# Turning q in 64x64 transposes for two more groups, and two stores sent out as one transfer each

## The chip, the cores and the metric

The kernel runs on one core of a Trainium2 chip. A core has five engines, each with its own queue of instructions: TensorE (PE in the profile, with its weight loads as PEld), VectorE (DVE), ScalarE (ACT), GpSimd (POOL) and SyncE (SP). SP only issues transfers; 16 DMA engines carry these out. The engines wait for each other and for transfers by semaphores. The metric is the device time of one execution in microseconds (us); less is better. The numbers of a profile come from one profiled execution, the times from runs of their own.

## The reference: linear attention, then a gated channel mix

The inputs q, k and v have 8 batches, 8 heads, 576 positions and 64 columns in float32. The two stages, cut to their core:

```python
# attention
q_s = softmax(q, over the 64 columns)
k_s = softmax(k, over the 576 positions)
kv  = einsum('bhsd,bhse->bhde', k_s, v)
x   = einsum('bhsd,bhde->bhse', q_s, kv)      # then heads side by side: [8, 576, 512]
# channel mix
xk = mu_k * x + (1 - mu_k) * x_prev           # x_prev: x one position earlier, zero at first
xr = mu_r * x + (1 - mu_r) * x_prev
k  = relu(xk @ w_k)                           # 512 -> 1024
v  = (k * k) @ w_v                            # 1024 -> 512
out = sigmoid(xr @ w_r) * v
```

## The kernel before

**Attention by groups.** Four heads of one batch make a group, so there are 16 groups, written (b, g) with batch b from 0 to 7 and g 0 or 1. A tile of a group holds two heads side by side in its 128 partitions (64 each) and nine blocks of 64 columns for each of two head pairs; position 9p + j stands in partition p, block j. For each group ACT takes the exponentials of q and k, DVE sums and scales q to `qs`, and ACT casts v. TensorE then needs q turned, with the 64 columns of a head along the partitions, because the product with kv contracts over them.

**Three ways of turning q.** Groups of batches 5 to 7 (`CROSSBAR`) turn it with a transposing transfer that SP issues (L516). All others use TensorE: `transpose_q` (L362 to L369) multiplies by an identity. Its loop runs over the nine blocks j, over column parts `u` and over the two partition halves `r`. For groups named in `WHOLE` (L36) there is one part of 128 columns, so 18 transposes that use 64 rows and all 128 columns of the array. For the others there are two parts of 64 columns, so 36 transposes, each in a quarter of the array. The result is the same. The halves r go to two banks of PSUM, from where ACT copies the turned q to `qt` (`copy_qt`).

**Blocks on TensorE.** From batch 1 on, the transposes and the 36 products of `kv` (L396) for one group form one block of TensorE's queue. Where the group before has its x still to compute, those products (L536, tile `w` and `qt`) are put ahead into the same block, named B; a block without them is named TKV. The first groups of batches 2 and 3 have TKV blocks (TKV20 and TKV30), the second ones B blocks (B21 and B31). The x of the last group stands alone as X71; it reads `qt_c`, which the crossbar transfer qt71 writes.

**Channel mix by units.** The 4608 rows of x are worked in ten units of 512 or 256 positions. A unit has eight products with w_k (k.., L620), ReLU on ACT (L607), a square on DVE (L611), and then for each tile m of 128 rows: the gate's product (r.., L652), tanh on ACT into a buffer `th` (L657), the product with w_v (v.., L672), and on DVE the gating into the same buffer (o.., L678). The stores (st.., L688) follow.

**A tile's stores.** The first 64 partitions of a tile hold one column block j of a batch and the last 64 the next one. In the output their rows lie nine rows apart, so the function `store` sends each half on its own: 64 rows of 2 KB, 128 KB. A tile of unit 6 has the stores st60 and st60.2, st61 and st61.2, and so on. All go through SP's queue, but for some of the last unit, which ACT issues.

**What sets the order.** Nothing is scheduled automatically. `graph` makes the operations with their dependencies; the text `ORDER` lists every operation's name, with the number of the buffer that it takes after a colon, and each engine runs its operations in that order. There are seven `th` buffers (a to g). In unit 6 the tile st60 is in th_b, st61 in th_f, st62 in th_e and st63 in th_g. SP's order there is: st60, st61, st62, st63 (two transfers each), the crossbar transfer qt71, and then unit 7's stores. th_f and th_e are taken again by unit 8's tanh.

The lines that the change meets:

```python
WHOLE = ((0, 0), (0, 1), (1, 0), (1, 1), (2, 0), (3, 0))
...
for u in ((slice(0, 128),) if (b, g) in WHOLE else two):
...
jb = (RING * half + c) // 64 + i
bb, j = jb // J, jb % J
dst = bass.AP(tensor=kn.out.tensor, offset=kn.out.offset + (bb * S + j) * C + part.start,
              ap=[[J * C, 64], [1, width]])
```

Of the kernel before, what the change touches and what calls it, by code (L numbers as in the profile page):

```python
# [16 lines left out]
B, H, S, D = 8, 8, 576, 64  # L17
C = H * D
F = 1024
J = S // 64  # L20
CT = C // 128
FT = F // 128
RING = 4 * S
# [9 lines left out]
XO = 368  # L33

FILLS = 22
WHOLE = ((0, 0), (0, 1), (1, 0), (1, 1), (2, 0), (3, 0))  # L36
FUSED = (0, 1)
EARLY_UNITS = 2
ALONE = ((2, 1), (B - 1, 1))
CROSSBAR = tuple((b, g) for b in range(5, B) for g in range(2))  # L40
FIRST = ((0, 0), (0, 1), (1, 0), (1, 1))

ORDER = """
# [57 lines left out]
sc6010:1 relu64:1 mix600 k66:0 sq62 edge61 relu65:2 sq63 k67:2 diff61:0 relu66:0 r60:1 sq64  # L101
sc6100:2 relu67:1 sc6101 r61:3 sq65 th60:1 mix610 v600:0 sq66 th61:5 sc6011 sq67 v610:2 sc6110:0
sc6111 mix601 v601 mix611 v611 rz70:2 w70:1 r62:1 o60 o61 st60 r63:3 th62:4 st60.2 v620:0 st61
th63:6 st61.2 v630:2 v621 v631 o62 k70:1 st62 o63 st62.2 k71:3 relu70:2 st63 st63.2 k72:0 sq70:1
relu71:0 qt71:2 k73:2 sq71 relu72:1 k74:1 sq72 relu73:2 k75:3 sq73 relu74:0 k76:0 sq74 relu75:1
k77:2 sq75 relu76:2 r70:1 sq76 relu77:0 B71:0.1 sq77 th70:0 v700:3 xb70:0 rz71:0 w71:2 r71:0 v701
th71:3 xs70 v710:2 o70 edge70 X71:1.0 st70 diff70:1 v711 xb71:1 st70.2 sc7000:2 r72:1 sc7001 xs71
o71 r73:0 edge71 st71 th72:2 mix700 st71.2 v720:3 diff71:0 th73:1 sc7010:1 v730:2 sc7100:0 sc7101
sc7110:2 v721 mix710 sc7111 v731 sc7011 o72 k80:1 mix711 st72 k81:0 st72.2 o73 relu80:1 mix701
st73 k82:3 relu81:2 st73.2 sq80:0 k83:2 sq81 relu82:0 k84:1 sq82 relu83:1 k85:0 sq83 relu84:2  # L110
k86:3 sq84 relu85:0 k87:2 sq85 relu86:1 r80:1 sq86 relu87:2 r81:0 sq87 th80:5 v800:3 th81:4 v810:2
v801 v811 o80 r82:1 st80 o81 st80.2 r83:0 th82:6 st81 st81.2 v820:3 th83:0 v830:2 v821 v831 o82
k90:1 st82 o83 k91:0 st82.2 relu90:0 k92:3 st83 relu91:1 sq90:1 k93:2 relu92:2 sq91 st83.2 k94:1
relu93:0 sq92 k95:0 relu94:1 sq93 k96:3 relu95:2 sq94 k97:2 relu96:0 sq95 r90:1 relu97:1 sq96 sq97
r91:0 th90:3 v900:3 th91:2 v901 v910:2 o90 v911 st90.2 st90 v910.2:1 o91 v911.2 st91.2 st91 o91.2
st91.4 st91.3
"""


# [16 lines left out]
class Plan:  # L136
# [6 lines left out]
    def add(self, engine, emit, deps=(), takes=(), gives=(), name=""):  # L143
        self.names[name] = self.names.get(name, 0) + 1
        if self.names[name] > 1:
            name = f"{name}.{self.names[name]}"
        op = Op(engine, emit, deps, takes, gives, name)
        self.ops.append(op)
        return op
# [29 lines left out]
def graph(kn):  # L179

    plan = Plan()
    add = plan.add
# [93 lines left out]
    def emit_rest():  # L276
# [10 lines left out]
        out=kn.mu[:], in_=kn.bank(mu_slot)[:, 0:8]), [mu_mm], [], [mu_slot], name="mucopy")  # L287
# [10 lines left out]
    def weight(dst, src, n, ct, step, count, col):  # L298
# [5 lines left out]
                    name=f"wk{h}{g}") for g in range(2)] for h in range(2)]  # L304
    wr_done = add("POOL", lambda: weight(kn.wr, kn.w_r, C, 0, 1, CT, 0), name="wr")
    wv_done = [add("POOL", lambda i=i, a=a, e=e: weight(kn.wv[i], kn.w_v, C, a, 1, e - a, 0),
                   name=f"wv{i}") for i, (a, e) in enumerate(zip(WV, WV[1:]))]
# [7 lines left out]
    def attention(b, g):  # L315
# [46 lines left out]
        def transpose_q(slot):  # L362
            for j in range(J):
                for u in ((slice(0, 128),) if (b, g) in WHOLE else two):
                    for r in range(2):
# [58 lines left out]
        for n, u in enumerate(us):  # L424
# [7 lines left out]
            elif n == 0:  # L432
                castv.append(vdone[g])
        crossed = (b, g) in CROSSBAR
        before_t, before_kv = scaled + [identity], expk + castv + [consts]
# [155 lines left out]
    def wv_of(ft):  # L591
        i = max(i for i in range(3) if WV[i] <= ft)
        return kn.wv[i][:, ft - WV[i]]

    def unit(half, c0, n, index):
# [30 lines left out]
        for f0 in range(0, FT, 4 if early else 1):  # L626
            step = 4 if early and f0 == 0 else 1
            for f1 in range(f0, f0 + (4 if early else 1), step):
                kfs = [Slot("mm") for _ in range(step)]
                mms = [None] * step  # L630
                for cts in ((0, 2), (1, 3)) if step == 4 else ((0, 2, 1, 3),):
                    gs = sorted({ct % 2 for ct in cts})
                    for i in range(step):
# [5 lines left out]
                                     name=f"k{index}{fc}")  # L639
# [5 lines left out]
        for m in range(tiles):  # L645
            c = c0 + 128 * m
            rps, th = Slot("mm"), Slot("th")
            parts = [slice(0, 256), slice(256, 512)] if last and m == tiles - 1 else [slice(0, C)]

            def r_part(rps=rps, c=c):  # L650
                for ct in range(CT):
                    kn.nc.tensor.matmul(kn.bank(rps), lhsT=kn.xs[1][:, ct, c:c + 128],  # L652
                                        rhs=kn.wr[:, ct, :], start=(ct == 0),
                                        stop=(ct == CT - 1))

            def tanh(rps=rps, th=th):
                kn.nc.scalar.activation(out=kn.ths[th.index][:], in_=kn.bank(rps),  # L657
                                        func=ACT.Tanh, scale=0.5)

            own = sorted({4 * half + c // S, 4 * half + (c + 127) // S})  # L660
            r = add("PE", r_part,
                     [o for b in own for g in range(2) for o in mixed[b, g, 1]] + [wr_done],
                     [rps], [], name=f"r{index}{m}")
            rdone.append(r)
            t = add("ACT", tanh, [r], [th], [rps], name=f"th{index}{m}")
            for part in parts:
                vps = Slot("mm")
                width = part.stop - part.start

                def v_part(fts, vps=vps, m=m, part=part, width=width):  # L670
                    for ft in fts:
                        kn.nc.tensor.matmul(kn.bank(vps)[:, 0:width],  # L672
                                            lhsT=kn.k2s[k2.index][:, ft, 128 * m:128 * m + 128],
                                            rhs=wv_of(ft)[:, part], start=(ft == 0),
                                            stop=(ft == FT - 1))

                def gated(vps=vps, th=th, part=part, width=width):
                    kn.nc.vector.scalar_tensor_tensor(  # L678
                        out=kn.ths[th.index][:, part], in0=kn.ths[th.index][:, part],
                        scalar=1.0, in1=kn.bank(vps)[:, 0:width], op0=ALU.add, op1=ALU.mult)  # L680

                def store(i, queue, th=th, c=c, part=part, width=width):
                    jb = (RING * half + c) // 64 + i
                    bb, j = jb // J, jb % J
                    dst = bass.AP(tensor=kn.out.tensor,
                                  offset=kn.out.offset + (bb * S + j) * C + part.start,
                                  ap=[[J * C, 64], [1, width]])
                    kn.queues[queue].dma_start(  # L688
                        out=dst, in_=kn.ths[th.index][64 * i:64 * (i + 1), part])

                o = None
                cuts = WV if index == 0 else (0, 4, 8)
                for h, (a, e) in enumerate(zip(cuts, cuts[1:])):
                    o = add("PE", lambda v=v_part, a=a, e=e: v(range(a, e)),
                             squares[a:e] + [o or r] + [wv_done[i] for i in range(3)
                                                        if WV[i] < e and WV[i + 1] > a],
                             [] if a else [vps], [k2] if e == FT else [], name=f"v{index}{m}{h}")
                o = add("DVE", gated, [o, t], [], [vps], name=f"o{index}{m}")
                for i in range(2):
                    queue = "ACT" if last and m >= tiles - 2 and i else "SP"  # L700
                    add(queue, lambda i=i, q=queue, f=store: f(i, q), [o], [], [th],
                        name=f"st{index}{m}")
        units_of[half, c0] = (bs, kdone, rdone)

    index = 0
    for half in range(B // 4):
        for c0, n in UNITS:
            unit(half, c0, n, index)
            index += 1
# [128 lines left out]
```

## Time and profile before

| what | number |
|---|---|
| median of 3 runs | 196.36 us (195.99 to 196.37) |
| the profiled execution's own time | 195.85 us |
| its span, first to last instruction | 194.1 us |
| TensorE busy | 185.5 us (96%), 1849 products |
| VectorE, ScalarE, GpSimd busy | 150.0, 140.5, 43.6 us |
| DMA | 41.86 MB, mean 216 GB/s |
| chain that ended last | PE 77%, DMA 15%, POOL 2%, ACT 2%, issue 1% |

A busy share is over the whole span. A row of a timeline gives start, duration, engine, line, operation, tiles (out<-in), the part of the array used (rows*columns), the shape and how many. TensorE's products are pipelined, so a group's row reaches into the next one's; how long a group holds the queue is read from one start to the next. On SP a row is the issue of a transfer, not the transfer itself. The share of DMA in a stretch is the mean over 16 engines of the time that their packets took.

### The profile page before, as it was taken

The page shows a single profiled execution, that of the slowest core. Times are in us where ns is not written, and L with a number is a line of the kernel's source. Part 1 is how long each engine was busy: PE and PEld are TensorE (multiplying, and loading weights), DVE is VectorE, ACT ScalarE, POOL GpSimd, SP SyncE. Part 2 cuts the span into 40 slices and gives each one's busy share as a digit, 9 for nine tenths or more (in the row PEclk, how much of TensorE's full clock was granted, in tenths as well). Part 3 has the DMA queues.
Part 4 walks back from the last instruction along what each step waited for, and adds up shares of the span by engine and source line. Part 5 has one row for each costly group of instructions (what it writes and reads, how often), then busy time and mean ns, then how long its engine had stood idle before and what let it go on. Part 6 is the DMA issues. An engine that isn't in the chain of part 4 may idle for free.

```text
span 194.1 us, 4743 instructions
## 1 busy us (share of the span) xinstructions
PE 185.5 (96%) x1849; PEld 90.6 (47%) x1873; DVE 150.0 (77%) x347; ACT 140.5 (72%) x218; POOL 43.6 (22%) x70
## 2 busy tenths in 40 slices
PE   7989999999999999999999999999999999999991
PEld 2264445435544554554554444444444444444751
DVE  1897668799999999999989998999924469622531
ACT  3687889899999999989996798767225641752440
POOL 8444357794414212241110000000000000000000
PEclk9999999999999999999999999999999999999999
DMA  6999999999999998899699504786049122404413
GB/s 205 312 265 289 269 349 303 400 394 393 411 391 394 392 414 339 290 351 326 145 229 120 205 0 107 163 200 147 0 110 138 34 54 54 111 0 98 93 27 108
DMA packets 23646, 41.86 MB, mean 216 GB/s; under 512 B 9404, under 2 KB 12744, under 8 KB 23624
## 3 DMA queue, kind: packets, MB, share of 16 engines
q0 software_dynamic: 9440, 27.99, 45.3%
q1 hardware_dynamic: 13368, 12.13, 25.8%
q10 hardware_dynamic: 816, 1.44, 2.0%
q8 instruction: 14, 0.23, 0.5%
q14 instruction: 8, 0.07, 0.1%
HBM read 33.56 MB, written 9.44 MB: 222 GB/s over the span
## 4 chain that ended last, share of the span: by engine, by line
PE 77%; DMA 15%; POOL 2%; ACT 2%; issue 1%; DVE 0%; POOLq 0%
PE mm_c L672 10%; PE mm_d L672 9%; PE mm_c L620 8%; PE mm_b L620 7%; PE mm_a L620 7%; PE mm_b L652 7%; PE mm_d L620 6%; DMA wk_ab<-in_moe_w_k_dram 6%; PE mm_a L672 5%; DMA wv_a<-in_moe_w_v_dram 5%; PE mm_b L672 4%; DMA raw_k<-in_v_dram 4%; PE mm_a L652 4%; PE mm_d L652 3%; PE mm_c L652 1%
## 5 line engine op out<-in xcount | busy, mean ns | idle before, releaser
L672 PEld LDWEIGHTS <-k_a 128*128 128x128 bf16 x144 | 13.7, 98 | 16.7 <-issue 0.5
L652 PEld LDWEIGHTS <-xr 128*128 128x128 bf16 x144 | 13.9, 98 | 16.2 <-issue 0.2
L672 PEld LDWEIGHTS <-k_b 128*128 128x128 bf16 x152 | 14.4, 98 | 15.0 <-issue 0.2
L652 PE MATMUL mm_b<-wr,xr 128*128 128x512 bf16 x62 | 16.3, 379 | 0.1
L620 PEld LDWEIGHTS <-wk_ab 128*128 128x128 bf16 x80 | 7.6, 97 | 8.3 <-issue 0.8
L620 PEld LDWEIGHTS <-wk_bb 128*128 128x128 bf16 x80 | 7.8, 98 | 7.7
L620 PEld LDWEIGHTS <-wk_aa 128*128 128x128 bf16 x80 | 7.4, 98 | 8.2 <-issue 0.9
L620 PEld LDWEIGHTS <-wk_ba 128*128 128x128 bf16 x80 | 7.5, 98 | 7.9 <-DMA wk_ba<-in_moe_w_k_dram 0.2
L652 PE MATMUL mm_a<-wr,xr 128*128 128x512 bf16 x35 | 9.2, 380 | 0.1
L672 PE MATMUL mm_c<-wv_a,k_a 128*128 128x512 bf16 x32 | 8.2, 379 | 0.0
L607 ACT ACTIVATE rel_b<-mm_b 128x512 bf16<-128x512 f32 (+1 forms) x7 | 4.0, 572 | 4.9 <-PE mm_b L620 4.8
L607 ACT ACTIVATE rel_a<-mm_b 128x512 bf16<-128x512 f32 (+1 forms) x8 | 4.6, 570 | 3.9 <-PE mm_b L620 3.6
L620 PE MATMUL mm_c<-xk,wk_aa 128*128 128x512 bf16 (+1 forms) x26 | 7.3, 363 | 0.0
L611 DVE TENSOR_TENSOR k_a<-rel_b 128x512 bf16<-128x512 bf16 (+1 forms) x14 | 5.3, 380 | 2.5 <-ACT rel_b L607 2.5
L672 PE MATMUL mm_d<-wv_a,k_b 128*128 128x512 bf16 x26 | 7.1, 379 | 0.1
L652 PE MATMUL mm_d<-wr,xr 128*128 128x512 bf16 x28 | 7.2, 379 | 0.0
L620 PE MATMUL mm_c<-xk,wk_ab 128*128 128x512 bf16 (+1 forms) x24 | 6.9, 362 | 0.0
L611 DVE TENSOR_TENSOR k_b<-rel_a 128x512 bf16<-128x512 bf16 (+1 forms) x14 | 5.5, 391 | 1.8 <-ACT rel_a L607 1.3
L607 ACT ACTIVATE rel_c<-mm_a 128x512 bf16<-128x512 f32 (+1 forms) x11 | 6.0, 550 | 0.7 <-PE mm_a L620 0.7
L611 DVE TENSOR_TENSOR k_b<-rel_b 128x512 bf16<-128x512 bf16 (+1 forms) x14 | 5.5, 391 | 1.3 <-ACT rel_b L607 0.9
L611 DVE TENSOR_TENSOR k_b<-rel_c 128x512 bf16<-128x512 bf16 (+1 forms) x12 | 4.7, 391 | 1.9 <-ACT rel_c L607 1.6
L620 PE MATMUL mm_d<-xk,wk_bb 128*128 128x512 bf16 (+1 forms) x22 | 6.1, 360 | 0.1
(352 smaller groups left out, 532.5 us busy)
## 6 DMA issues: line engine op xcount, KB each, us to landing
out_dram<-th_b SPq DMA_DIRECT2D x12, 128.0 KB, 3.8
out_dram<-th_g SPq DMA_DIRECT2D x12, 128.0 KB, 2.4
out_dram<-th_d SPq DMA_DIRECT2D x11, 128.0 KB, 8.7
out_dram<-th_a SPq DMA_DIRECT2D x10, 128.0 KB, 2.8
out_dram<-th_f SPq DMA_DIRECT2D x10, 128.0 KB, 2.4
raw_k<-in_v_dram POOLq DMA_DIRECT2D x2, 576.0 KB, 9.0
raw_c<-in_q_dram POOLq DMA_DIRECT2D x2, 576.0 KB, 7.0
raw_b<-in_q_dram POOLq DMA_DIRECT2D x2, 576.0 KB, 10.3
```

Of the source, the lines that this page charges most:

```text
L607: kn.nc.scalar.activation(out=kn.rels[rel.index][:, 0:n], in_=kn.bank(kf)[:, 0:n], func=ACT.Relu, scale=HALF_ROOT)
L611: kn.nc.vector.tensor_tensor(out=kn.k2s[k2.index][:, fc, 0:n], in0=kn.rels[rel.index][:, 0:n], in1=kn.rels[rel.index][:, 0:n], op=ALU.mult)
L620: kn.nc.tensor.matmul(kn.bank(kf)[:, 0:n], lhsT=kn.wk[fc // 4][ct % 2][:, ct // 2, (fc % 4) * 128: (fc % 4) * 128 + 128], rhs=kn.xs[0][:, ...
L652: kn.nc.tensor.matmul(kn.bank(rps), lhsT=kn.xs[1][:, ct, c:c + 128], rhs=kn.wr[:, ct, :], start=(ct == 0), stop=(ct == CT - 1))
L672: kn.nc.tensor.matmul(kn.bank(vps)[:, 0:width], lhsT=kn.k2s[k2.index][:, ft, 128 * m:128 * m + 128], rhs=wv_of(ft)[:, part], start=(ft == ...
```

## The change

Two edits. First, (2, 0) and (3, 0) leave `WHOLE`, so the blocks TKV20 and TKV30 turn q in 36 transposes of 64x64 instead of 18 of 64x128. Second, tiles (6, 1) and (6, 2), unit 6's second and third, are sent out by a new function `store_both`: one transfer of 128 rows instead of two of 64. Its destination has three levels, two column blocks, 64 rows and 512 columns; its source is the whole tile. In `ORDER` the names st61.2 and st62.2 go, and the last two stores, one on SP's queue and one on ACT's, change places. The rest of the text is only wrapped anew.

```diff
-WHOLE = ((0, 0), (0, 1), (1, 0), (1, 1), (2, 0), (3, 0))
+WHOLE = ((0, 0), (0, 1), (1, 0), (1, 1))
...
+MERGED = ((6, 1), (6, 2))
...
-th63:6 st61.2 v630:2 v621 v631 o62 k70:1 st62 o63 st62.2 k71:3 relu70:2 st63 st63.2 k72:0 sq70:1
+th63:6 v630:2 v621 v631 o62 k70:1 st62 o63 k71:3 relu70:2 st63 st63.2 k72:0 sq70:1 relu71:0 qt71:2
...
-r91:0 th90:3 v900:3 th91:2 v901 v910:2 o90 v911 st90.2 st90 v910.2:1 o91 v911.2 st91.2 st91 o91.2
-st91.4 st91.3
+th90:3 v900:3 th91:2 v901 v910:2 o90 v911 st90.2 st90 v910.2:1 o91 v911.2 st91.2 st91 o91.2 st91.3
+st91.4
...
                 o = add("DVE", gated, [o, t], [], [vps], name=f"o{index}{m}")
+
+                def store_both(th=th, c=c):
+                    jb = (RING * half + c) // 64
+                    bb, j = jb // J, jb % J
+                    assert j + 1 < J
+                    dst = bass.AP(tensor=kn.out.tensor, offset=kn.out.offset + (bb * S + j) * C,
+                                  ap=[[C, 2], [J * C, 64], [1, C]])
+                    kn.nc.sync.dma_start(out=dst, in_=kn.ths[th.index][:])
+
+                if (index, m) in MERGED:
+                    add("SP", store_both, [o], [], [th], name=f"st{index}{m}")
+                    continue
                 for i in range(2):
```

More of the change, by code (lines that the diff above doesn't have):

```diff
@@ L103 @@
 sc6111 mix601 v601 mix611 v611 rz70:2 w70:1 r62:1 o60 o61 st60 r63:3 th62:4 st60.2 v620:0 st61
-th63:6 st61.2 v630:2 v621 v631 o62 k70:1 st62 o63 st62.2 k71:3 relu70:2 st63 st63.2 k72:0 sq70:1
[L105 to L114, printed above, removed]
@@ L115 @@
-r91:0 th90:3 v900:3 th91:2 v901 v910:2 o90 v911 st90.2 st90 v910.2:1 o91 v911.2 st91.2 st91 o91.2
-st91.4 st91.3
+th63:6 v630:2 v621 v631 o62 k70:1 st62 o63 k71:3 relu70:2 st63 st63.2 k72:0 sq70:1 relu71:0 qt71:2
+k73:2 sq71 relu72:1 k74:1 sq72 relu73:2 k75:3 sq73 relu74:0 k76:0 sq74 relu75:1 k77:2 sq75
+relu76:2 r70:1 sq76 relu77:0 B71:0.1 sq77 th70:0 v700:3 xb70:0 rz71:0 w71:2 r71:0 v701 th71:3 xs70
+v710:2 o70 edge70 X71:1.0 st70 diff70:1 v711 xb71:1 st70.2 sc7000:2 r72:1 sc7001 xs71 o71 r73:0
@@ new lines @@
+edge71 st71 th72:2 mix700 st71.2 v720:3 diff71:0 th73:1 sc7010:1 v730:2 sc7100:0 sc7101 sc7110:2
+v721 mix710 sc7111 v731 sc7011 o72 k80:1 mix711 st72 k81:0 st72.2 o73 relu80:1 mix701 st73 k82:3
+relu81:2 st73.2 sq80:0 k83:2 sq81 relu82:0 k84:1 sq82 relu83:1 k85:0 sq83 relu84:2 k86:3 sq84
+relu85:0 k87:2 sq85 relu86:1 r80:1 sq86 relu87:2 r81:0 sq87 th80:5 v800:3 th81:4 v810:2 v801 v811
+o80 r82:1 st80 o81 st80.2 r83:0 th82:6 st81 st81.2 v820:3 th83:0 v830:2 v821 v831 o82 k90:1 st82
+o83 k91:0 st82.2 relu90:0 k92:3 st83 relu91:1 sq90:1 k93:2 relu92:2 sq91 st83.2 k94:1 relu93:0
@@ L117 @@
+sq92 k95:0 relu94:1 sq93 k96:3 relu95:2 sq94 k97:2 relu96:0 sq95 r90:1 relu97:1 sq96 sq97 r91:0
+th90:3 v900:3 th91:2 v901 v910:2 o90 v911 st90.2 st90 v910.2:1 o91 v911.2 st91.2 st91 o91.2 st91.3
+st91.4
 """
```

## The prediction

> **What bounds the kernel now.** I read the page first (busy shares, slices), then TensorE's timeline around the four first groups, then SP's timeline and the stretches table around unit 6's stores.
>
> ```profile
> span 194.1 us, 4743 instructions
> PE 185.5 (96%) x1849; PEld 90.6 (47%) x1873; DVE 150.0 (77%) x347; ACT 140.5 (72%) x218; POOL 43.6 (22%) x70
> PE   7989999999999999999999999999999999999991
> ```
>
> TensorE (PE) is busy at 90% or more in every slice from the fourth to the last but one, at full granted clock. Each microsecond that its queue saves after 10 us moves the end, unless a later wait takes it back; each microsecond that it waits is added. The listing of PE from 64 to 190 us shows idle only in three gaps of 0.16 us, each where a group of four shows one record fewer, so no wait is visible there.
>
> TensorE's timeline, both kinds of transposing (start, duration of the group, what):
>
> ```profile
> 45.89 1.03 PE L652 MATMUL mm_b<-wr,xr 128*128 128x512 bf16 x4
> 46.85 0.44 PE L366 MATMUL att_a<-ident,qs_b 64*128 64x64 bf16 x18
> 47.22 0.48 PE L396 MATMUL att_a<-vv_c,ek_b 64*64 64x65 bf16 x36
> 47.63 1.04 PE L652 MATMUL mm_a<-wr,xr 128*128 128x512 bf16 x3
> ...
> 50.23 1.03 PE L672 MATMUL mm_b<-wv_a,k_b 128*128 128x512 bf16 x4
> 51.18 0.22 PE L536 MATMUL att_b<-qt_b,w_a 64*64 64x64 bf16 x4
> 51.24 0.39 PE L536 MATMUL att_a<-qt_b,w_a 64*64 64x512 bf16 x4
> 51.46 0.46 PE L366 MATMUL att_b<-ident,qs_c 64*64 64x64 bf16 x36
> 51.74 0.47 PE L396 MATMUL att_b<-vv_a,ek_c 64*64 64x65 bf16 x36
> 52.15 1.04 PE L672 MATMUL mm_c<-wv_a,k_b 128*128 128x512 bf16 x3
> ...
> 59.64 0.44 PE L366 MATMUL att_b<-ident,qs_a 64*128 64x64 bf16 x18
> 60.00 0.48 PE L396 MATMUL att_b<-vv_b,ek_a 64*64 64x65 bf16 x36
> ```
>
> Read the starts, since pipelined groups overlap. The rows at 46.85 and 59.64 are the two blocks that change (TKV20, TKV30): 18 transposes take 0.37 and 0.36 us to the next start. The row at 51.46 (B21) is already the new form: 36 transposes of 64x64 in 0.28 us. The three other such blocks, at 66.83, 71.37 and 85.42, take 0.30 each. The kv products behind take 0.41 after either form (47.22 to 47.63, 51.74 to 52.15).
>
> SP's timeline at unit 6's stores, and the PE rows that need the crossbar transpose behind them:
>
> ```profile
> 141.96 1.11 SPq L688 DMA_DIRECT2D out_dram<-th_f  x2
> 145.50 1.11 SPq L688 DMA_DIRECT2D out_dram<-th_e  x2
> 146.70 1.18 SPq L688 DMA_DIRECT2D out_dram<-th_g  x2
> 147.98 1.39 SPq L516 DMA_TRANSPOSE qt_c<-qs_a  x1
> ```
>
> ```profile
> 156.54 1.03 PE L672 MATMUL mm_c<-wv_a,k_b 128*128 128x512 bf16 x4
> 157.50 0.22 PE L536 MATMUL att_a<-qt_c,w_c 64*64 64x64 bf16 x4
> ```
>
> The rows th_f and th_e are the stores to be merged (st61, st62); th_g is st63; qt_c is qt71. The list of DMA issues gives qt71 4.6 us to landing, so 152.6. X71 reads it at 157.50: 4.9 us of slack.
>
> How fast rows move, by stretch (four busy columns, clock, DMA share, GB/s):
>
> ```profile
> 50.00:60.00 10.00, 9.95 (x143) 4.63 (x142) 9.64 (x22) 10.00 (x15) 2.97 (x5) 1.00 1.04 400
> 143.00:144.00 1.00, 1.00 (x6) 0.49 (x5) 0.00 (x0) 0.00 (x0) 0.00 (x0) 1.00 0.82 193
> ```
>
> Loads: 400 GB/s over 16 full engines is 25 GB/s each, 82 ns per 2 KB row. The pair th_f alone: 193/(16 x 0.82) = 14.7 GB/s per busy engine, 139 ns per row.
>
> **The change part by part.**
>
> *Transposes.* Removed: 2 x 18 transposes of 64x128, 0.37 and 0.36 us. Added: 2 x 36 of 64x64, at 0.28 to 0.30 us a block. Gain 0.06 to 0.09 each; I take 0.075, so 0.15 us for two. The unknown is the entry: B21 follows other 64x64 work, the changed blocks follow a full-array group. That entry costs the same to both forms as far as rows show: r to TKV20 is 0.96 us (45.89 to 46.85), v to X21 is 0.95 (50.23 to 51.18), where four full-array products without a change take 0.86 to 0.87. So 0.09 us in both; if the new form paid it twice, the gain would be 2 x (0.075 - 0.09), a loss of 0.03 us, and if the entry vanished, a gain of 2 x 0.165 = 0.33 us. These are the ends.
>
> [...]
>
> The blocks wait for the same scaled q, exponentials and cast v as before, and the copy, reciprocal and weights behind them (qt20, rz20, w20) only come sooner. No wait is added on PE, ACT or DVE, and the orders of ACT, DVE and POOL are unchanged.
>
> *Stores.* Four issues on SP become two. One store's issue is some 0.55 us (1.11 for two), the transpose's 1.39; the merged one's is not shown and lies between these, so two cost 1.1 to 2.8 us against 2.2. SP is idle between its rows th_f and th_e (143.07 to 145.50), so only th_e's issue reaches qt71: 0.6 us sooner to 0.3 later, nothing against 4.9 us of slack. Behind the merged issues on SP stand st63, qt71 and unit 7's stores. th_f and th_e are taken again by unit 8's first two tanh, after the product at 170.99 in the chain, long behind their landing. Bytes and rows (2 KB) stay the same. The swapped order of the last two stores changes nothing on an engine: one is on SP, the other on ACT.
>
> What a merged store does to the DMA engines is the open cost. Its destination is 2 x 64 x 512 with 2 outermost, where every store of before has 64 rows outermost. Either its rows are spread over 16 engines as now, and the cost is nothing; or they go to 2 engines, 64 rows each. Then th_f's rows start at 143.0 (the window from 141 us shows the first traffic of that pair 1.0 us after issue), and th_e's, th_g's share (4 + 4 rows an engine) and qt71's share queue behind them: 136 rows an engine. qt71's own transfer takes between 1.4 us (its two busy stretches, 149 to 150 and 151 to 152, less the gap) and 3.4 (last store row near 149.2 to landing 152.6). At 82 ns: 143.0 + 11.2 + 1.4 to 3.4 = 155.6 to 157.6, against 157.5: hidden, just (0.1 us late at worst). At 139 ns: 163.3 to 165.3, a PE stall of 5.8 to 7.8 us. I take 82 ns: with two engines alone there is no crowd of 16 at the source, and the loads' engines keep that rate for tens of microseconds. So this part costs 0, and both ends go into the range.
>
> *Sum.* -0.15 + 0 us. The profiled execution took 195.85 us (span 194.1 and 1.75 around it), 0.51 below the median of 196.36. So 195.70 against its own time, and 196.2 as a median: 0.08% faster, which the runs' own spread (195.99 to 196.37) would hide. About 0.2% (0.39 us) is what a measurement of this kernel can tell from no change.
>
> **The rivals.**
>
> *Slower: the merged rows hold up qt71.* Place: X71 on PE at 157.5. It decides when a row takes over (157.5 - 143.0 - 3.4)/136 = 82 ns with the long tail, or 96 ns with the short one. For it: the 139 ns seen on stores, and that PE has nothing else in its order to run. Against: 82 ns seen on loads, and an early landing leaves room. A slightly slow row (90 to 110 ns) stalls PE up to 3.9 us, most likely 0.5 to 2.5: 196.7 to 198.7. At 139 ns: 202.0 to 204.0.
>
> [...]
>
> *Slower: 36 small transposes cost twice 18.* At the old blocks' 20 ns each they take 0.73 us, a loss of 2 x 0.365 = 0.73: 197.1. Against it stand four blocks in this trace at 0.28 to 0.30.
>
> *Spread over 16 engines anyway.* The merge then does nothing for the end; same time as the forecast.
>
> *Faster by over 0.2%.* The entry cost vanishes (0.33 us) and the runs fall on the good side, or SP's saved issues free something that I don't see: 195.8.
>
> **How the numbers follow.** Forecast with the store hidden, on 2 engines or 16: 0.55. Small stall at X71: 0.17. Large stall: 0.14. Transposes dearer: 0.04. Faster: 0.10. So faster 0.10, same 0.55, slower 0.35. Range: low 195.6 (the 0.33 us gain and 0.4 of spread), high 199.0, which takes in the small stall and leaves out the large one. The forecast's own range is 195.8 to 196.6. Predicted 196.2.
>
> **What would show it.** After, 36 rows of 64*64 at some 46.85 and 59.57, with kv 0.28 to 0.30 behind, and every later PE row 0.15 sooner. SP with one row th_f and one th_e. Landing of a merged store: about 2.4 us says 16 engines; 6 to 7 for th_f and 8 to 9 for th_e say 2 engines at 82 ns; 10 or more says slow rows. PE without idle before att_a<-qt_c (X71) says that the store is hidden; a wait there for the DMA qt_c<-qs_a, with its time added to the span, proves me wrong. If the new transposes take over 0.37 us, the first part is wrong.

## The result, and the profile after

The changed kernel takes 196.61 us (median of 22 runs, 196.22 to 198.19) against 196.10 us for the kernel before (22 runs beside them, 195.80 to 197.43). The ratio of the means is 1.0029, with a 95% interval of 1.0017 to 1.0042: slower by 0.29%, some 0.57 us. The forecast was 0.08% faster.

The page of the changed kernel's profile (span, busy shares, TensorE's slices, and the queue that brings PE its instructions):

```profile
span 194.9 us, 4811 instructions
PE 185.3 (95%) x1885; PEld 91.0 (47%) x1909; DVE 149.6 (77%) x347; ACT 140.8 (72%) x218; POOL 43.6 (22%) x70
PE   7699999999999989999999999999999999999992
q8 instruction: 15, 0.25, 0.5%
```

In the page of the kernel before, that last line reads:

```profile
q8 instruction: 14, 0.23, 0.5%
```

TensorE has 36 products more, and its instructions come in one packet more of 16 KB (0.25 MB / 15). Little else on this page moved. Its own time was 196.72 us.

TensorE's timeline of the changed kernel, the two blocks that were changed (TKV20 and TKV30):

```profile
47.45 0.48 PE L367 MATMUL att_a<-ident,qs_b 64*64 64x64 bf16 x36
47.75 0.47 PE L397 MATMUL att_a<-vv_c,ek_b 64*64 64x65 bf16 x36
...
60.16 0.48 PE L367 MATMUL att_b<-ident,qs_a 64*64 64x64 bf16 x36
60.47 0.47 PE L397 MATMUL att_b<-vv_b,ek_a 64*64 64x65 bf16 x36
```

The blocks hold the queue for 0.30 and 0.31 us, where 0.37 and 0.36 stood before. To compare the two traces, take the start of the same row in both. The changed kernel is 0.60 us late at TKV20 already, which is a slower start of this one execution and lies ahead of either edit (in eight other traces that change nothing ahead of it, TKV20 starts between 47.16 and 47.86; the 46.85 before is the early one). Behind TKV20 it is 0.53 late (47.75 against 47.22), behind TKV30 0.47 (60.47 against 60.00). So the transposes gained 0.12 us, about as forecast. Eleven microseconds later that is lost, and more. The same view, at the block B40 (the x of group (3, 1), then q and kv of group (4, 0)), which the change doesn't touch:

```profile
71.84 0.48 PE L367 MATMUL att_b<-ident,qs_c 64*64 64x64 bf16 x36
72.13 0.39 PE L397 MATMUL att_b<-vv_a,ek_c 64*64 64x65 bf16 x24
73.12 0.29 PE L397 MATMUL att_b<-vv_a,ek_c 64*64 64x65 bf16 x12 [0.60 <-issue]
73.34 1.04 PE L673 MATMUL mm_d<-wv_a,k_a 128*128 128x512 bf16 x3
```

and in the kernel before:

```profile
71.37 0.48 PE L366 MATMUL att_b<-ident,qs_c 64*64 64x64 bf16 x36
71.67 0.49 PE L396 MATMUL att_b<-vv_a,ek_c 64*64 64x65 bf16 x36
72.09 1.04 PE L672 MATMUL mm_d<-wv_a,k_a 128*128 128x512 bf16 x3
```

The tiles qs_c, vv_a and ek_c are those that `ORDER` gives to group (4, 0); where the expectations below speak of the second group of batch 3, they mean this block. The 36 kv products are one run without a wait in the program. Before, they take 0.42 us. Now PE stops after the 24th of them, and the run takes 1.21 us. The releaser is "issue": PE waited for nothing that the profile shows. The lateness jumps from 0.47 to 1.25 us here and stays there (X71: 158.75 against 157.50; last row: 190.92 against 189.66).

The stores. SP's timeline of the changed kernel, then the PE rows that need the crossbar transfer:

```profile
143.23 0.60 SPq L707 DMA_DIRECT2D out_dram<-th_f  x1
146.75 0.52 SPq L707 DMA_DIRECT2D out_dram<-th_e  x1
147.61 1.20 SPq L689 DMA_DIRECT2D out_dram<-th_g  x2
148.90 5.31 SPq L517 DMA_TRANSPOSE qt_c<-qs_a  x1
```

```profile
157.79 1.03 PE L673 MATMUL mm_c<-wv_a,k_b 128*128 128x512 bf16 x4
158.75 0.22 PE L537 MATMUL att_a<-qt_c,w_c 64*64 64x64 bf16 x4
```

The list of DMA issues of the changed kernel (issues, median us to landing), and its stretches table, first in the rows of th_f, then in those of th_e behind them (the last two columns are DMA share and GB/s):

```profile
out_dram<-th_g SPq DMA_DIRECT2D x2, 128.0 KB, 8.9
qt_c<-qs_a SPq DMA_TRANSPOSE x1, 9.3
```

```profile
145.00:147.00 2.00, 2.00 (x11) 0.89 (x10) 0.79 (x2) 0.00 (x0) 0.00 (x0) 1.00 0.12 33
...
153.00:155.00 2.00, 1.95 (x45) 0.89 (x45) 0.93 (x3) 1.47 (x3) 0.00 (x0) 1.00 0.13 51
```

A DMA share of 0.12 of 16 engines is two engines, 17 GB/s each, some 120 ns for a row of 2 KB; later the two move 51 GB/s, some 80 ns a row. The trace's semaphore records say the same: an unmerged store's semaphore takes sixteen steps as it lands (143.94 to 144.20 for the first half of th_f before), that of the merged th_f one at 144.25, early, and two as it lands, at 151.29 and 151.33, 8.1 us after issue, and that of th_e two at 156.43 and 156.46, 9.7 us after issue. So th_e's 64 rows an engine took 5.1 us behind th_f's, 80 ns each. The crossbar transfer lands 9.3 us after its issue instead of 4.6, at 158.2. PE needs it at 158.75 and doesn't wait: hidden, with 0.5 us to spare.

The end. The last TensorE row and ACT's last issues of the kernel before (span 194.1), then of the changed one (span 194.9):

```profile
189.66 0.38 PE L672 MATMUL mm_b<-wv_c,k_b 128*128 128x256 bf16 x2
189.75 1.40 ACTq L688 DMA_DIRECT2D out_dram<-th_c  x2
```

```profile
190.92 0.38 PE L673 MATMUL mm_b<-wv_c,k_b 128*128 128x256 bf16 x2
191.01 1.40 ACTq L689 DMA_DIRECT2D out_dram<-th_c  x2
```

To two digits the spans are 194.07 and 194.95. From the start of that last row to the end of the span it is 4.41 us before and 4.03 after, with the same rows between: 0.38 us are gained behind all the work. The profiled spans add up: +0.60 (start) - 0.12 (transposes) + 0.78 (stop) - 0.38 (end) = +0.88 us, as 194.95 - 194.07. Without the start's share the edits make +0.28 us in these two executions.

### The profile page after: what moved, and what is told of

Its sections match the earlier page's. It is cut to its first block, busy times and chain, and to the rows that moved or that the text cites. A ratio compares the mean times of both kernels' runs of the same rounds, so it can differ in the third digit from the quotient of the medians.

```text
span 194.9 us, 4811 instructions
## 1 busy us (share of the span) xinstructions
PE 185.3 (95%) x1885; PEld 91.0 (47%) x1909; DVE 149.6 (77%) x347; ACT 140.8 (72%) x218; POOL 43.6 (22%) x70
## 4 chain that ended last, share of the span: by engine, by line
PE 90%; DMA 3%; issue 2%; DVE 2%; ACT 1%; ACTq 0%; DVEq 0%
PE mm_c L673 11%; PE mm_d L673 10%; PE mm_c L621 9%; PE mm_b L621 8%; PE mm_a L621 8%; PE mm_d L621 7%; PE mm_b L653 7%; PE mm_a L673 6%; PE mm_b L673 5%; PE mm_a L653 4%; DMA raw_c<-in_q_dram 3%; PE mm_d L653 3%; PE mm_c L653 2%; PE att_a L397 1%; PE att_b L397 1%
```

## The experiments

Each ratio below compares a run with runs of the kernel before taken beside it, whose medians lie between 196.17 and 196.39 us; times of two groups of experiments are compared by their ratios.

**Transposes alone, and stores alone.**

```diff
 t_only: the kernel before, with
-WHOLE = ((0, 0), (0, 1), (1, 0), (1, 1), (2, 0), (3, 0))
+WHOLE = ((0, 0), (0, 1), (1, 0), (1, 1))
 m_only: the changed kernel, with WHOLE as before
```

> Only the transposes are changed (36 of 64x64 in the first groups of batches 2 and 3); all stores are as before. Theory P: TensorE's queue is fed in blocks of instructions, and the 72 added ones move the end of a block into the kv products of the second group of batch 3, where the queue runs dry for some 0.8 us. Then this kernel stops there as the changed one did (about 73 us, some 0.8 us between two of the 36 products) and takes 0.4 to 0.7 us over before. Theory S: the loss is the merged stores', and the transposes gain what their rows say: then 0.15 us under before, with no stop there.

> Only the two stores of unit 6 are merged; all transposes are as before. Theory P: the merged stores are hidden, so within 0.1 us of before, with the crossbar transfer behind them landing about 9 us after issue, just ahead of its reader. Theory S: 0.5 to 0.7 us over before, with TensorE stopped ahead of X71.

t_only: 197.37 us, ratio 1.0054 (1.0034 to 1.0073). TensorE's timeline has the stop:

```profile
72.21 0.39 PE L396 MATMUL att_b<-vv_a,ek_c 64*64 64x65 bf16 x24
73.38 0.29 PE L396 MATMUL att_b<-vv_a,ek_c 64*64 64x65 bf16 x12 [0.79 <-issue]
73.60 0.39 PE L672 MATMUL mm_d<-wv_a,k_a 128*128 128x512 bf16 x1
```

1.39 us for the run instead of 0.42. m_only: 196.21 us, 0.9995 (0.9977 to 1.0013), without a stop in the kv products. So the slowdown comes with the transposes, at a place that they are not in. In m_only's profiled execution the crossbar transfer took 10.8 us to landing, and PE did stop for it (the row names DVE as releaser, which had long been done):

```profile
158.81 0.22 PE L537 MATMUL att_a<-qt_c,w_c 64*64 64x64 bf16 x4 [0.92 <-DVE xd_b L555]
```

The merged stores' cover is thin: 9.3 us is hidden, 10.8 us is not.

**More instructions, no transposes.** What the transposes add is 72 instructions on PE's queue, 36 products and 36 weight loads. The theory that the queue runs dry says that any 72 will do.

```diff
 b_pad72: the kernel before, with a NoOp behind each of the first 72 full-array products
+    def padded(mm):
+        for _ in range(min(1, kn.pad)):
+            kn.nc.tensor.nop(hint="pad", nofuse=True)
+            kn.pad -= 1
+        return mm
...
-                kn.nc.tensor.matmul(kn.bank(kf)[:, 0:n],
+                padded(kn.nc.tensor.matmul(kn.bank(kf)[:, 0:n],
...
+    kn.pad = 72
```

> The kernel before with 72 empty instructions (no operation) in TensorE's queue, one behind each of the first 72 full-array products, so that the blocks of instructions end where they do in the changed kernel from the second group of batch 3 on; no transpose and no store is changed. Theory P: the stop of some 0.8 us in that group's kv products appears here too, and the kernel takes 0.5 to 0.9 us over before. Theory S, or a stop that belongs to the small transposes themselves: no stop, and within 0.2 us of before.

197.38 us, 1.0052 (1.0031 to 1.0074). The same stop after the same 24 products, in a kernel that computes as before does:

```profile
71.88 0.39 PE L396 MATMUL att_b<-vv_a,ek_c 64*64 64x65 bf16 x24
72.93 0.29 PE L396 MATMUL att_b<-vv_a,ek_c 64*64 64x65 bf16 x12 [0.66 <-issue]
```

**Shifting the boundary on.** PE's instructions come in packets of 16 KB (16384 bytes each in the trace's records). In the changed kernel 15 of them bring some 3800 instructions, so about 256 a packet, 64 bytes each. Take the stop behind the 24th kv product of B40 as the end of a block of 256 and count from there in the queue's order. In the kernel before that block ends elsewhere and is used up in 9.7 us; in t_only 112 of its 128 products are small ones of B31 and B40, and PE gets through it in 5.0 us. More NoOps move the boundary off.

```diff
 t_pad184: t_only, with two NoOps behind each of the first 92 full-array products
 t_pad84:  t_only, with one behind each of the first 84
 t_pad84b: t_pad84 once more
 after_pad84: the changed kernel, with the same 84
```

> The changed transposes alone, with 184 empty instructions in TensorE's queue, two behind each of the first 92 full-array products: 72 and 184 make 256, so that from the second group of batch 3 on the blocks of instructions end where they do in the kernel before. Theory P: no stop in that group's kv products, and 0.0 to 0.2 us under before, if the empty instructions cost nothing beside the products. A stop that belongs to the small transposes: it stays, 0.4 to 0.7 us over before.

> The changed transposes alone, with 84 empty instructions in TensorE's queue, one behind each of the first 84 full-array products. Counted on the trace of t_only, no stretch of 256 instructions in the loading phase is then used up in less than 5.7 us, where the stretch that ran dry was used up in 5.0 (5.8 with the stop). Theory P: no stop in any kv products, and 0.1 to 0.2 us under before (0.9990 to 0.9995). A stop that belongs to the small transposes, or to the number of added instructions and not to their place: 0.4 us or more over before.

> The same kernel as t_pad84, once more. Theory P: the transposes' own gain, 0.1 to 0.2 us under before (0.9990 to 0.9995), and no stop.

> Both edits, as in the changed kernel, with the 84 empty instructions of t_pad84. Theory P: no stop in any kv products; the loss of the changed kernel is gone, 0.1 us under before, or up to 0.3 us over where the crossbar transfer behind the merged stores lands late (0.9990 to 1.0015). If the two edits together cost something of their own: 0.5 us or more over before.

t_pad184 has no stop at B40, but 197.97 us, 1.0076 (1.0060 to 1.0092): the expectation for the time missed. The NoOps themselves, two for each product, use up a block so fast that PE stops at its end, early in the loads:

```profile
34.39 0.38 PE L678 MATMUL mm_d<-wv_b,k_a 128*128 128x512 bf16 x1
36.48 0.39 PE L678 MATMUL mm_d<-wv_b,k_a 128*128 128x512 bf16 x1 [1.71 <-issue]
```

The mechanism made at another place, at 1.7 us. In the queue's order this stop lies 1024 instructions ahead of t_only's, four times 256, so both are block ends. With 84 single NoOps neither stop is there (t_pad84):

```profile
72.50 0.49 PE L396 MATMUL att_b<-vv_a,ek_c 64*64 64x65 bf16 x36
72.92 1.04 PE L678 MATMUL mm_d<-wv_a,k_a 128*128 128x512 bf16 x3
```

0.42 us again, and 195.96 us, 0.9990 (0.9967 to 1.0013); the repeat 196.01 us, 0.9995 (0.9973 to 1.0017). Between t_only and these lies nothing but 84 instructions that do nothing, and about 0.6% of the time. after_pad84, both edits and no stop: 195.73 us, 0.9972 (0.9949 to 0.9996), faster than both kernels.

**Why the refill is late.** In t_only PE enters the block at 67.56 us, the next block's packet runs from 71.04 to 72.14, and PE goes on at 73.38. In the six traces with such a stop the packet starts 3.1 to 4.3 us after PE has entered the block at hand, and PE goes on 1.2 to 1.6 us behind the packet's end. If it queues behind the loads of q, k and v, which fill the DMA engines there, lighter loads must cure it with the boundary where it was.

```diff
 t_light: t_only, with loads of batches 4 to 7 of four column blocks instead of nine
+                n = J * D if b < 4 else 4 * D
...
-                             ap=[[J * D, 128], [4 * S * D, u.stop - u.start], [1, J * D]])
-                return kn.queues[op.engine].dma_start(out=kn.raws[slot.index][:, u, :], in_=ap)
+                             ap=[[J * D, 128], [4 * S * D, u.stop - u.start], [1, n]])
+                return kn.queues[op.engine].dma_start(out=kn.raws[slot.index][:, u, 0:n], in_=ap)
```

> The changed transposes alone, but the loads of batches 4 to 7 bring only four of a tile's nine column blocks (so the second half of the result is computed from other numbers); all else as t_only, the instructions and their blocks too. If the block of instructions came late since the DMA engines were full of loads: the 16 KB packet that came at 71.0 us in t_only comes sooner after the queue has passed the block's end, and the stop of 0.8 us in the kv products of the second group of batch 3 is gone or under 0.3 us. If the block comes late for a reason of the queue itself: the stop stays.

The stretches tables of t_only and of t_light (first column PE's busy time, last two DMA share and GB/s):

```profile
70.00:72.00 2.00, 2.00 (x28) 0.85 (x30) 1.97 (x5) 2.00 (x5) 0.00 (x0) 1.00 1.04 407
72.00:74.00 2.00, 1.21 (x77) 0.87 (x71) 1.92 (x6) 2.00 (x4) 0.16 (x1) 1.00 1.04 406
```

```profile
66.00:70.00 4.00, 4.00 (x96) 2.08 (x94) 3.81 (x10) 4.00 (x7) 1.19 (x2) 1.00 0.99 324
70.00:72.00 2.00, 2.00 (x11) 0.92 (x10) 1.99 (x4) 2.00 (x4) 0.14 (x1) 1.00 0.72 239
72.00:74.00 2.00, 2.00 (x86) 1.15 (x84) 1.95 (x5) 2.00 (x4) 0.00 (x0) 1.00 0.04 14
```

With the engines no longer full all the time PE runs on (2.00 of 2.00, against 1.21), with the same instructions in the same blocks. The refill packet came at 69.6 us, 1.2 us after PE had entered the block, against 71.0 and 3.5 us in t_only. Its single time, 197.15 us, says nothing here, since it has fewer loads; the stop does.

**Half of the transposes.**

```diff
 t_one: the kernel before, with
+WHOLE = ((0, 0), (0, 1), (1, 0), (1, 1), (3, 0))
```

> Only the first group of batch 2 turns q in 36 transposes; the first group of batch 3 keeps 18, and the stores are as before. 36 more instructions, so by the same count the stretch that ran dry now ends behind the kv products of the second group of batch 3 and lasts some 6.2 us. Theory P: no stop, 0.05 to 0.1 us under before. If each changed group has a price of its own: half of t_only's loss, 0.5 us over before.

No stop in the kv products, the new block at 0.30 us (47.84 to 48.14). The time, 196.87 us, 1.0021 (0.9999 to 1.0044), doesn't tell the expected 0.05 to 0.1 us from nothing, nor from the 0.5 us over of the other case. This run settles only that 36 instructions more don't put a boundary at the bad place.

**A third merged store.**

```diff
 m_three: m_only, with
-MERGED = ((6, 1), (6, 2))
+MERGED = ((6, 1), (6, 2), (6, 3))
```

> Three merged stores in unit 6 (the second, third and fourth tile), all transposes as before. If a merged store runs on two DMA engines, as the slow flow of 33 GB/s in the changed kernel says, the third adds 64 rows of 80 ns an engine, less the 8 rows of th_g that were there, so 4.5 us to the landing of qt71: some 13 to 15 us after issue, and TensorE stops 3.5 to 5 us ahead of X71: 1.018 to 1.026. If the slow flow has another cause and the merge is harmless: within 0.3 us of before.

202.54 us, 1.0322 (1.0289 to 1.0354): more than the 1.018 to 1.026 expected. PE's row at X71, and its stretches table behind it (the third column from the end is the granted clock):

```profile
162.56 0.22 PE L537 MATMUL att_a<-qt_c,w_c 64*64 64x64 bf16 x4 [4.05 <-DMA qt_c<-qs_a]
```

```profile
162.50:164.00 1.50, 1.44 (x11) 0.51 (x12) 0.00 (x0) 0.77 (x1) 0.00 (x0) 0.56 0.01 3
164.00:166.00 2.00, 2.00 (x6) 0.71 (x5) 0.95 (x3) 0.41 (x2) 0.00 (x0) 0.50 0.00 0
166.00:168.00 2.00, 2.00 (x10) 0.89 (x9) 2.00 (x6) 1.19 (x2) 0.00 (x0) 0.98 0.49 114
```

The transfer took 14.5 us to landing and the stop is 4.05 us, both as expected. What I missed: after it PE ran for some 3.4 us at half clock, another 1.65 us. This is the rival that the prediction feared; two merged stores lie at its edge, with no stop in the changed kernel's profile and 0.92 us in m_only's.

**The changed kernel again.**

```diff
 after_again: the changed kernel, unchanged
```

> The changed kernel once more, beside the others on one chip. Theory P: the stop at 72 to 74 us, and 0.3 to 1.0 us over before, as t_only within the intervals. If the merged stores gave back part of t_only's loss, it would stay 0.4 us or more under t_only's 1.0054.

196.92 us, 1.0047 (1.0018 to 1.0077), and the stop again:

```profile
73.36 0.29 PE L397 MATMUL att_b<-vv_a,ek_c 64*64 64x65 bf16 x12 [0.75 <-issue]
```

**The end of the span.** By now all kernels with merged stores ended 4.03 to 4.11 us behind the start of TensorE's last row, and all without 4.40 or 4.41 (the expectations below work with spans rounded to 0.1 us). With that gain the changed kernel should be only 0.3 to 0.5 us slower. Four runs took this apart. The trace's records of SP's last instructions (the time at which each wait was passed, in us, and in brackets which of eight semaphores it looks at; the transfers that SP and ACT issue use these in turn) read:

```
before:  192.75 (0)  192.81 (1)  192.88 (2)  192.94 (3)  193.00 (4)  193.06 (5)  193.12 (6)  193.18 (7)  193.25 drain
after:   192.36 (0)  192.43 (1)  193.02 (2)  193.08 (3)  193.58 (4)  193.65 (5)  193.99 (6)  194.05 (7)  194.11 drain
```

SP ends with one wait for each of these, in this order, 0.062 us apart if all are over. Before, the last store to land uses number 0, so the whole row is still to do when its wait is passed at 192.75: 0.50 us to the drain. Two transfers fewer (88 instead of 90) shift the turn by two, the last store to land uses number 6, and 0.13 us are left.

```diff
 m_unit7: m_only, merged at another unit, the last two stores in the order of before
-MERGED = ((6, 1), (6, 2))
+MERGED = ((7, 0), (7, 1))
 b_split6: the kernel before, with three tiles' stores of unit 5 cut in half, six transfers more
+SPLIT = ((5, 0), (5, 1), (5, 2))
...
+                if (index, m) in SPLIT:
+                    for i in range(2):
+                        for cut in (slice(0, 256), slice(256, 512)):
+                            add("SP", lambda i=i, f=store, p=cut: f(i, "SP", part=p, width=256),
+                                [o], [], [th], name=f"st{index}{m}")
+                    continue
 a_unit7: both edits, merged stores as in m_unit7
 best7: a_unit7, with the 84 NoOps
```

> Transposes as before; the merged stores are not tiles 1 and 2 of unit 6 but tiles 0 and 1 of unit 7, behind which no crossbar transfer stands on SP; the order of the last two stores is that of before. In the traces so far the span ends 4.44 us after the start of TensorE's last row before the change and 3.98 to 4.13 us after it in every kernel with merged stores (4.36 to 4.44 in every kernel without). Theory E: SP ends with ten waits that look at the transfers' semaphores two at a time, 0.062 us each, and two transfers less shift which of the eight semaphores the last store uses, from the second wait to the eighth, so six waits of 0.062 us lie beside the stores instead of behind them: end distance 4.05, the time 0.37 us under before, ratio 0.9981. With no crossbar transfer behind the merged rows there is no stop of TensorE. Rival M: the end distance is shorter because merged rows of unit 6 thin out the last stores, or for the swapped order of the last two; then 4.4 and ratio 1.000.

> The kernel before, with the stores of unit 5's tiles 0 to 2 cut in half along the columns: six transfers more, none merged, same bytes. Six more shift the eight semaphores just as two less do. Theory E: end distance 4.05 us instead of 4.44 and 0.37 us under before, ratio 0.9981, if six more issues on SP (0.55 us each, where SP is mostly idle) stay hidden. Rival M: end distance 4.4, ratio 1.000 or above.

> Both edits, but the merged stores at unit 7, tiles 0 and 1. The stop in the kv products stays as in the changed kernel (0.8 to 1.0 us). Sum by theory E: -0.16 for the transposes, +0.8 to 1.0 for the stop, -0.37 at the end, so 0.27 to 0.47 us over before, ratio 1.0014 to 1.0024. The changed kernel itself measured 1.0029 and 1.0047. If this one comes out 0.2 us or more under those, the rest is what the crossbar transfer costs behind the merged stores in some executions; if it is as slow, the stop is larger in the timed executions than in the profiled ones.

> As a_unit7, and with the 84 NoOps on TensorE that took the stop out of the kv products. No stop there and none at X71. Sum: -0.16 for the transposes and -0.37 at the end, ratio 0.9973, as after_pad84 had with the merged stores at unit 6 (0.9972); 0.1 to 0.2 us better than that if the crossbar transfer was late in some of its executions.

b_split6: 195.83 us, 0.9972 (0.9947 to 0.9996). It merges nothing, issues six transfers more, and is faster. The distance from its last PE row to the end of its span (194.93) is 4.03 us:

```profile
190.90 0.38 PE L673 MATMUL mm_b<-wv_c,k_b 128*128 128x256 bf16 x2
```

m_unit7: 195.88 us, 0.9977 (0.9948 to 1.0006), distance 4.04; the time alone would not show it, the distance does. In both the last store to land uses number 6, and in m_three, with three transfers fewer, number 5, with 4.11 us. So the gain is the count of transfers modulo eight; the merged rows and the swapped order are not needed for it. a_unit7: 197.24 us, 1.0039 (1.0009 to 1.0070), not below the changed kernel: nothing speaks for a late crossbar transfer as what is left over, though 0.2 us would be lost in this interval. best7: 195.84 us, 0.9974 (0.9944 to 1.0003), as after_pad84.

a_unit7's profile shows a second loss, at 108 us. ACT waits for a load of k, the tanh queued behind that wait comes late, and PE waits for the tanh:

```profile
106.74 1.16 ACT L328 ACTIVATE ek_a<-raw_f 128x1152 bf16<-128x1152 f32 x1 [1.44 <-DMA raw_f<-in_k_dram]
```

```profile
108.44 0.59 PE L621 MATMUL mm_b<-xk,wk_aa 128*128 128x512 bf16 x2 [0.97 <-ACT th_g L658]
```

The load took 9.1 us to landing, in after_again 9.1 (a stop of 1.03 us) and in b_pad72 8.7 (0.63 us). In the other fourteen traces it took 5.2 to 7.5 us and nothing stopped, the changed kernel's first trace among them (6.9). So three of the five traces with the stop in the kv products have a late load, and none of the twelve without it. The three executions took 197.78 to 198.14 us, the other two 196.72 and 197.37.

## Why the prediction was wrong

**The transposes: right.** Forecast 0.15 us, measured 0.12 us, with blocks of 0.30 and 0.31 us. The dearer-transposes rival (0.73 us a block) is off: 36 starts in 0.30 us are 8 ns each.

**"No wait is added on PE, ACT or DVE": the step that failed.** No wait was added in the program, and PE still waits. The first reading, that each microsecond saved in the queue moves the end "unless a later wait takes it back", priced only waits for other engines and transfers. PE's queue of instructions is itself supplied by transfers (q8 on the page: 15 packets in 0.25 MB). The 72 instructions more put the end of a 256-instruction block into the kv products of B40, and the block ahead of it holds nearly nothing but short products, so PE empties it in 5.0 us; beside full DMA engines the next block's packet starts only 3.2 us after PE has entered this one, ends 1.1 us later, and PE goes on another 1.4 us later. Cost: 0.78 us in the changed kernel's profile, 0.97 in t_only's. Shown by three turns: 72 NoOps make it (b_pad72), 84 take it away with the transposes in place (t_pad84, twice), and lighter loads take it away with the boundary in place (t_light).

**"So this part costs 0": right at X71, wrong at the end.** The stores do go to two engines, as the DMA share of 0.12 and the two steps at landing show; before, it was one of two cases that I could only price. The rate lies between my ends: some 120 ns a row for th_f, about 80 ns (50 GB/s over two engines) for th_e behind it. That I took 82 ns since two engines meet no crowd at the source was an estimate that no run shows: th_f's rows had two engines alone, and ran at 120 ns. The crossbar transfer came at 158.2 in an execution that runs 1.25 us late, so at 156.95 on the forecast's scale, where I had 155.6 to 157.6; PE needed it at 157.50 on that scale. That it fell inside is partly luck: the store rows took 12.8 us where I had 11.2, and the crossbar transfer's own part took 1.1 us behind them where I had 1.4 to 3.4. The landings of 8.1 and 9.7 us lie between my signs for 82 ns and for slow rows. "Hidden, just" was the right verdict for the changed kernel's profile; m_only's, with 0.92 us of stop, shows how just. Two things were missing. SP's issue of the crossbar transfer took 5.31 us instead of 1.39 (10.27 in m_three, behind three merged stores; why was not shown); nothing behind it on SP was due. And that the swapped order "changes nothing on an engine" was true, but two transfers fewer change which semaphore the last store uses: 0.37 us by SP's waits, 0.38 us in the spans, the largest gain of the whole change.

**The sum.** -0.12 + 0.78 - 0.38 = +0.28 us in the profiles, where I had -0.15. Measured: +0.57 us (0.33 to 0.82). The rest, 0.05 to 0.54 us, is not settled. A second stop of 0.6 to 1.0 us at 108 us in a part of the executions would fill it; three of the five profiles with the first stop show it, but a profile is one execution, and whether the late load follows from the first stop was not tried. The range (195.6 to 199.0) held the result by luck: the chance for slower (0.35) was placed on the merged rows (0.31) and dearer transposes (0.04), and the cause was one that no rival named.

## What to carry to other kernels

An edit that changed the number of TensorE's instructions moved the later block boundaries of its queue here (72 more made a stop of 0.60 to 0.79 us, 84 on top took it away): count where the boundaries fall, and look for one behind a stretch of short instructions while loads fill the DMA engines (5.0 us for the block here, beside some 400 GB/s). A stop with the releaser "issue" in the middle of a run without waits is the sign, and a few NoOps beside long products, which were not seen to cost anything (84 of them: 0.9990 and 0.9995), test it and cure it. When a time differs, compare the end of the span as well: here the number of transfers, modulo eight, was worth 0.4 us.

## What the runs showed that was not expected

- PE's instructions came in 16 KB packets, and beside loads at 400 GB/s the next one came late: 0.6 to 0.8 us of idle time behind a block used up in 5.0 us, none behind the blocks of 7.3 to 10.6 us that the kernel before has from 32 to 88 us. In the six such stops PE went on 1.2 to 1.6 us behind the end of the packet.
- After a stop of 4.05 us PE's granted clock was 0.5 for about 3.4 us, which cost 1.65 us more; the stops of 0.6 to 1.7 us were followed by full clock.
- Two DMA engines moved 33 GB/s in the first merged store, some 120 ns for a row of 2 KB, but about 50 GB/s in the one queued behind it. The crossbar transfer issued behind them held SP for 5.31 us (1.39 before), and for 10.27 us in m_three.
- SP's closing waits cost 0.062 us each, and which semaphore the last store used decided whether they lay beside it or behind it: 0.50 us against 0.13.
